# Two blocks of cached attention on one core: the order of the loads on SP's ring

## The chip, the cores and the metric

The kernel runs on one core of one Trainium2 chip. Its engines are named as the profile names them: PE (TensorE), ACT (ScalarE), DVE (VectorE), POOL (GpSimd) and SP (SyncE, which here only issues loads). The metric is the device time of one execution in microseconds. The time before is the median of three runs; one further execution was profiled.

## The reference, cut to what matters

Two problems, A and B, of the same shape and with separate inputs are computed one after the other, and their outputs stand side by side. For each:

```python
# x [16, 144, 448], k_cache and v_cache [16, 16, 512, 256], wq [448, 4096], wo [4096, 448], bf16
q = (x @ wq).reshape(B, Sq, H, Dh).transpose(0, 2, 1, 3)
scores = einsum("bhqd,bhkd->bhqk", q, k_cache) * (Dh ** -0.5)
p = softmax(scores, axis=-1)
o = einsum("bhqk,bhkd->bhqd", p, v_cache)
out = o.transpose(0, 2, 1, 3).reshape(B, Sq, H * Dh) @ wo
```

## The kernel before

The work is cut into 512 **units**, one for each problem, batch and head (256 per problem). For a unit U, PE does Q (L937: eight matmuls, x times the head's columns of wq), S (L961: eight, transposed scores, keys on the partitions), PV (L1007: eight, V times the exponentials) and one matmul with ones that sums the exponentials over the keys (L1019; it occurs once per unit, so that it counts units in the trace). ACT takes the exponential of S (L973) and the reciprocal of the sums as a logarithm and an exponential (L1030, L1035). POOL adds the exponentials of four key blocks to one before the sums matmul (L982, L986). DVE copies Q out of PSUM (L949), reduces the sums to a range flag (L1063) and writes the normalized result into `ring` (L1050), a buffer of four chunks of 128 output rows. The softmax takes no maximum off; the range flag at the end decides whether a second, general program (`_general_path`) runs instead, which these inputs don't need.

The output projection (L1098) takes a chunk of 128 rows of `ring` through all 32 blocks of `wo`, two matmuls at a time, paced by a credit: each unit adds `OP_RATE` matmuls to it, and a chunk can begin `OP_DELAY` units after its last batch is done. ACT copies a finished chunk out (L1116), and POOL stores it (L1127).

Every load is issued by SP, in one order, on one ring. K comes in **groups** of four units (1 MB) by a transposing DMA (`t_load_k`, L913) into one of `NK` slots; V in groups of four units by a plain DMA of 1 MB (`t_load_v`, L922) into one of `NV` slots. x comes for four batches at a time by two transposing DMAs (`t_load_x`, L903 and L904); wq in four pieces of four heads (`t_load_wq`, L882 and L884); wo in eight pieces (`t_load_wo`, L892). Because SP works in order, a load whose slot is not yet free holds up all loads behind it.

The whole program is written out by one loop over steps `i`. In step `i` the loads that are due are issued, and then come Q of unit `i + LQ`, S of unit `i + LS` and PV of unit `i`, followed by pieces of the output projection. Which load is issued in which step is decided by a plan: `plan()` notes for each load the earliest step `lo` (its slot is free), a deadline and a lead; the plan is sorted by deadline, and going through it in that order a load's step is the largest of the step of the load before it, its own `lo`, and its deadline less the lead. A group's K has a deadline two units ahead of its first unit, its V at its first unit; so K and V alternate. The second problem's wo pieces are not in the plan: each is issued when the last projection of problem A that reads the old piece has been written out.

Of the kernel before, what the change touches and what calls it, by code (L numbers as in the profile page):

```python
# [5 lines left out]
BF16 = mybir.dt.bfloat16  # L6
F32 = mybir.dt.float32
# [5 lines left out]
PE, ACT, DVE, POOL, SP = "pe", "act", "dve", "pool", "sp"  # L13
# [110 lines left out]
def _general_path(  # L124
# [45 lines left out]
    RC = RS * 128  # L170
    OP_DELAY = 2
    assert NT % 8 == 0
# [481 lines left out]
    while True:  # L654
# [51 lines left out]
        if 0 <= u < NT:  # L706
# [46 lines left out]
def bass_concat_heads__mha_block_cached__gqa_block_cached__near_ridge_kernel(  # L753
# [37 lines left out]
    assert NWO % WOG == 0 and WOG % OPP == 0 and NT % UG == 0  # L791
    NWG = NWO // WOG

    LQ, LS = 15, 2
    LDQ = SP
    NK, NV, NXG = 5, 4, 3
    XB = 4 if Bn % 4 == 0 else (2 if Bn % 2 == 0 else 1)
    NQT, NPT, NPS, NRI, NOST = 18, 4, 3, 2, 3
    RS = 4
    RC = RS * 128  # L800
    OP_DELAY = 2
    NXGT = NP * Bn // XB
    LIM_EXP = 40

# [2 lines left out]
    with contextlib.ExitStack() as es:  # L807
        mem = contextlib.ExitStack()

        def sb(name, shape, dt):  # L810
            return mem.enter_context(nc.sbuf_tensor(name, shape, dt))
# [14 lines left out]
        ps_sb = sb("ps_sb", [128, NPS, SQ], BF16)  # L826
        ln_sb = sb("ln_sb", [128, NRI, SQ], F32)
        rinv_sb = sb("rinv_sb", [128, NRI, SQ], F32)
        run_sb = sb("run_sb", [1, 2, NT], F32)
        ost_sb = sb("ost_sb", [128, NOST, D], BF16)  # L830
        stat = sb("stat", [128, 4], F32)
        flag_sb = sb("flag_sb", [128, 4], I32)
# [5 lines left out]
        S = _Sched()  # L838
# [38 lines left out]
        def t_load_wq(pr, hg):  # L877
            cols = slice(hg * 4 * DH, (hg + 1) * 4 * DH)
            w = wqs[pr]

            def e(q):
                q.dma_start(wq_sb[:, 0:3, cols], w[0:384, cols].rearrange("(c p) n -> p c n", p=128)).then_inc(  # L882
                    sems["wq%d" % hg], 16)
                return q.dma_start(wq_sb[64:128, 3, cols], w[384:448, cols]).then_inc(sems["wq%d" % hg], 16)  # L884
            S.add(LDQ, e, writes=[(("wq", hg), pr)], dma_sem="wq%d" % hg, n_dma=2, name="wq%d.%d" % (pr, hg))

        def t_load_wo(pr, wg):
            c0 = wg * WOG
            w = wos[pr]

            def e(q):
                return q.dma_start(wo_sb[:, c0:c0 + WOG, :],  # L892
                                   w[c0 * 128:(c0 + WOG) * 128, :].rearrange("(c p) n -> p c n", p=128)).then_inc(
                    sems["wo%d" % wg], 16)
            S.add(LDQ, e, writes=[(("wo", wg), pr)], dma_sem="wo%d" % wg, name="wo%d.%d" % (pr, wg))

        def t_load_x(XG):
            pr, j = divmod(XG, Bn // XB)
# [17 lines left out]
        def t_load_v(G):  # L916
            pr, b, h0 = unit(UG * G)
            sl = G % NV
            src = vs[pr][b, h0:h0 + UG].rearrange("u (p c) d -> p u (c d)", p=128)

            def e(q):
                return q.dma_start(v_sb[:, sl, :, :], src).then_inc(sems["v%d" % sl], 16)  # L922
            S.add(LDQ, e, writes=[(("v", sl), G)], dma_sem="v%d" % sl, name="v%d" % G)

        def t_q(U):
            pr, b, h = unit(U)
# [204 lines left out]
        t_init()  # L1131
        dma_plan = []

        def plan(lo, deadline, lead, fn, *args):
            dma_plan.append((deadline, len(dma_plan), lo, lead, fn, args))

        s_min = -LQ - 24
        for XG in range(NXGT):
            pr, j = divmod(XG, Bn // XB)
            u_first = pr * NU + j * XB * H  # L1140
            dl = u_first - LQ
            if XG >= NXG:
                pr0, j0 = divmod(XG - NXG, Bn // XB)
                lo = pr0 * NU + (j0 + 1) * XB * H - 1 - LQ + 1
            else:
                lo = s_min
            plan(lo, dl, 40, t_load_x, XG)
        for pr in range(NP):
            for hg in range(HG):
                dl = pr * NU + 4 * hg - LQ  # L1150
                lo = pr * NU - H + 4 * hg + 3 - LQ + 3 if pr > 0 else s_min
                plan(lo, dl, 10 ** 6, t_load_wq, pr, hg)
        for wg in range(NWG):
            plan(s_min, H - 4 + 2 * wg, 10 ** 6, t_load_wo, 0, wg)
        for G in range(NG):
            dl = UG * G - LS
            lo = UG * (G - NK) + UG - 1 - LS + 1 if G >= NK else s_min
            plan(lo, dl, 20, t_load_k, G)
        for G in range(NG):
            dl = UG * G  # L1160
            lo = UG * (G - NV) + UG - 1 + 3 if G >= NV else s_min
            plan(lo, dl, 12, t_load_v, G)
        dma_plan.sort(key=lambda t: t[:2])
        _prev = s_min
        _tmp = []
        for dl, sq, lo, lead, fn, args in dma_plan:
# [11 lines left out]
        tail_bank = {}  # L1178
# [5 lines left out]
        fifo = {"op": [], "qp": []}  # L1184
        stores = []
        credit = 0.0
        op_hold = -10 ** 9
        OP_RATE = float(NCH * NWO) / NU
        last_chunk_of = {pr: (pr + 1) * NCH - 1 for pr in range(NP)}
        flag_ev = None  # L1190

        def queue_chunk(r, ready):
            op_first[r], op_last[r] = 0, NWO - 1
            for c in range(NWO):
                fifo["op"].append((r, c, ready))
# [9 lines left out]
        i = s_min  # L1205
        while True:
            while dma_plan and dma_plan[0][0] <= i:
                _sl, _dl, _sq, fn, args = dma_plan.pop(0)
                fn(*args)
            while stores and stores[0][1] <= i:  # L1210
                t_store(stores.pop(0)[0])
            u = i + LQ
            if 0 <= u < NT:
                t_q(u)
                t_evac_q(u)
            u = i + LS
            if 0 <= u < NT:
                t_s(u)
                t_exp(u)
                t_presum(u)  # L1220
            u = i
            if 0 <= u < NT:
                t_pv(u)
                t_sum(u)
                t_recip(u)
                t_check(u)
                t_evac_ot(u)
                pr, b, h = unit(u)
# [113 lines left out]
```

## Time and profile before

| what | value |
|---|---|
| median of three runs | 1164.04 us (1160.04 to 1165.18) |
| the profiled execution, its own time | 1168.88 us |
| its span in the profile | 1167.0 us |
| granted PE clock, mean | 0.983 |
| DMA traffic, mean over the span | 252 GB/s, 294.21 MB |
| K load (transposing), median from issue to landing | 10.8 us (A), 10.6 us (B) |
| V load (plain), median from issue to landing | 6.3 us (A), 6.4 us (B) |

The page gives each engine's busy time as a share of the span. The span is the part of the execution that the trace covers. A wait is put down to the event that ended it. The DMA row of a window cuts it into 40 slices; in a window of 10 us a slice is 0.25 us, and its number is the GB/s that the ring's engines moved in it.

### The profile page before, as it was taken

Reading aid. Unit: us, or ns where it says so; the run is one execution under the profiler, and the core shown is the slowest. Engines: PE = TensorE matmul, PEld = TensorE weight load, DVE = VectorE, ACT = ScalarE, POOL = GpSimd, SP = SyncE. Lnnn points to the kernel's source line nnn. Section 1 sums busy time; section 2 is a strip of 40 time slices with the busy share of each in tenths; the row PEclk is TensorE's granted clock in tenths of the full one; section 3 lists DMA queues with packets and bytes.
Section 4 is the critical chain, followed back from the end, with each engine's and each line's share of the span. In section 5 each row is a group of like instructions: output and inputs, shape, how many; then the busy total and the mean of one; then the engine's idle time right before and its main releaser. Section 6 shows DMA issues by size and latency. Waiting matters only on the chain.

```text
span 1167.0 us, 33127 instructions
## 1 busy us (share of the span) xinstructions
PE 1059.2 (91%) x13952; PEld 928.1 (80%) x13952; DVE 655.6 (56%) x2183; ACT 621.5 (53%) x1573; POOL 642.0 (55%) x1065
## 2 busy tenths in 40 slices
PE   4988899988999989998789878999989998999995
PEld 3877888877897878887678767888878887888874
DVE  2554566555665656665346554666656665666543
ACT  0554556555665655655345444665646565556553
POOL 0554566555665656665346454666656665656553
PEclk9999999999999999999999999999999999999998
DMA  9999999999999999999999999999999999999992
GB/s 233 255 293 259 238 262 255 260 236 257 261 252 248 258 251 268 254 262 259 239 252 269 258 281 256 270 256 257 259 248 258 268 252 243 267 258 257 265 237 75
DMA packets 629087, 294.21 MB, mean 252 GB/s; under 512 B 550464, under 2 KB 558656, under 8 KB 628928
## 3 DMA queue, kind: packets, MB, share of 16 engines
q1 hardware_dynamic: 627200, 287.86, 108.9%
q0 software_dynamic: 1728, 4.13, 1.3%
q8 instruction: 111, 1.82, 0.7%
q14 instruction: 48, 0.39, 0.1%
HBM read 148.90 MB, written 4.13 MB: 131 GB/s over the span
## 4 chain that ended last, share of the span: by engine, by line
PE 57%; DMA 32%; SPq 5%; DVE 3%; ACT 1%; issue 1%; POOLq 0%; POOL 0%; ACTq 0%
DMA kt_sb<-in_B_k_cache_dram 15%; PE s_ps L961 15%; PE qp_ps L937 14%; PE ot_ps L1007 13%; PE op_ps L1098 13%; DMA kt_sb<-in_A_k_cache_dram 10%; DMA v_sb<-in_B_v_cache_dram 3%; SPq L903 2%; SPq L913 2%; PE ot_ps L1019 2%; DMA wq_sb<-in_B_wq_dram 1%; DMA v_sb<-in_A_v_cache_dram 1%; DVE qt_sb L949 1%; ACT pt_sb L973 1%; DVE run_sb L1063 1%
## 5 line engine op out<-in xcount | busy, mean ns | idle before, releaser
L982 POOL TENSOR_TENSOR pp_sb<-pt_sb 128x288 f32<-128x288 bf16 x512 | 373.5, 729 | 470.5 <-ACT pt_sb L973 469.6
L973 ACT ACTIVATE pt_sb<-s_ps 128x576 bf16<-128x576 f32 x512 | 332.8, 650 | 498.4 <-PE s_ps L961 498.4
L1063 DVE TENSOR_REDUCE run_sb<-ot_ps 1x1 f32<-1x144 f32 x1024 | 260.4, 290 | 429.5 <-ACT ln_sb L1030 429.5
L937 PEld LDWEIGHTS qp_ps<-xt_sb,wq_sb 128*128 128x128 bf16 x4096 | 293.0, 100 | 125.0 <-issue 24.9
L937 PE MATMUL qp_ps<-xt_sb,wq_sb 128*128 128x144 bf16 x4096 | 350.9, 231 | 40.5 <-DMA wq_sb<-in_A_wq_dram 11.1
L961 PE MATMUL s_ps<-qt_sb,kt_sb 128*128 128x144 bf16 x4096 | 345.2, 228 | 44.6 <-DMA kt_sb<-in_A_k_cache_dram 25.4
L1007 PE MATMUL ot_ps<-pt_sb,v_sb 128*128 128x144 bf16 x4096 | 343.4, 228 | 10.8 <-DMA v_sb<-in_B_v_cache_dram 7.9
L961 PEld LDWEIGHTS s_ps<-qt_sb,kt_sb 128*128 128x128 bf16 x4096 | 276.0, 99 | 57.0 <-DMA kt_sb<-in_A_k_cache_dram 29.6
L1007 PEld LDWEIGHTS ot_ps<-pt_sb,v_sb 128*128 128x128 bf16 x4096 | 276.7, 98 | 12.7 <-DMA v_sb<-in_B_v_cache_dram 8.7
L1098 PE MATMUL op_ps<-wo_sb,ring 128*128 128x448 bf16 x1120 | 281.9, 356 | 0.5 <-DVE ring L1050 0.5
L986 POOL TENSOR_TENSOR ps_sb<-pp_sb 128x144 bf16<-128x144 f32 x512 | 249.9, 488 | 40.1
L949 DVE CAST qt_sb<-qp_ps 128x288 bf16<-128x288 f32 x512 | 224.9, 439 | 70.1 <-PE qp_ps L937 67.3
L1050 DVE TENSOR_TENSOR ring<-ot_ps,rinv_sb 128x288 bf16<-128x288 f32 (+8 forms) x640 | 230.7, 375 | 0.0
L1035 ACT ACTIVATE rinv_sb<-ln_sb 128x144 f32<-128x144 f32 x512 | 165.4, 323 | 16.2
L1030 ACT ACTIVATE ln_sb<-ot_ps 128x144 f32<-128x144 f32 x512 | 148.6, 290 | 15.8 <-PE ot_ps L1019 15.8
L1098 PEld LDWEIGHTS op_ps<-wo_sb,ring 128*128 128x128 bf16 x1120 | 96.0, 99 | 29.5 <-issue 1.6
L1019 PE MATMUL ot_ps<-ps_sb,ones 128*128 128x144 bf16 x512 | 116.7, 228 | 0.0
L1019 PEld LDWEIGHTS ot_ps<-ps_sb,ones 128*128 128x128 bf16 x512 | 50.4, 98 | 0.0
L1127 POOL DMA_DIRECT2D out_dram<-ost_sb x36 | 20.2, 561 | 4.3 <-ACT ost_sb L1116 4.1
L1116 ACT ACTIVATE ost_sb<-op_ps 128x448 bf16<-128x448 f32 x35 | 18.6, 531 | 3.0 <-PE op_ps L1098 2.6
L1098 PE MATMUL qp_ps<-wo_sb,ring 128*128 128x448 bf16 x32 | 8.2, 353 | 0.0
L1098 PEld LDWEIGHTS qp_ps<-wo_sb,ring 128*128 128x128 bf16 x32 | 3.1, 98 | 2.7
(13 smaller groups left out, 6.1 us busy)
## 6 DMA issues: line engine op xcount, KB each, us to landing
v_sb<-in_A_v_cache_dram SPq DMA_DIRECT2D x64, 1024.0 KB, 6.3
v_sb<-in_B_v_cache_dram SPq DMA_DIRECT2D x64, 1024.0 KB, 6.4
out_dram<-ost_sb POOLq DMA_DIRECT2D x36, 112.0 KB, 6.2
wo_sb<-in_A_wo_dram SPq DMA_DIRECT2D x8, 448.0 KB, 5.9
wo_sb<-in_B_wo_dram SPq DMA_DIRECT2D x8, 448.0 KB, 4.6
wq_sb<-in_A_wq_dram SPq DMA_DIRECT2D x4, 768.0 KB, 8.2
wq_sb<-in_B_wq_dram SPq DMA_DIRECT2D x4, 768.0 KB, 8.5
kt_sb<-in_A_k_cache_dram SPq DMA_TRANSPOSE x64, 10.8
```

Of the source, the lines that this page charges most:

```text
L937: ins = t.matmul(qp_ps[:, dc * SQ:(dc + 1) * SQ], lhsT=wq_sb[:, kc, c0:c0 + 128], rhs=xt_sb[:, xsl, kc, xo:xo + SQ], start=(kc == 0 and dc ...
L949: return v.tensor_copy(qt_sb[:, sl, :, :], src)
L961: ins = t.matmul(s_ps[bank][:, c // 2, (c % 2) * SQ:(c % 2 + 1) * SQ], lhsT=kt_sb[:, ksl, 2 * c + dc, jj * 128:(jj + 1) * 128], rhs=qt_sb[ ...
L973: return a.activation(pt_sb[:, psl, :, :].rearrange("p (a b) q -> p a (b q)", a=2), s_ps[bank][:, :, 0:2 * SQ], AF.Exp, scale=DH ** -0.5)
L982: return g.tensor_tensor(pp_sb[:, sl, :, :], pt_sb[:, psl, 0:2, :], pt_sb[:, psl, 2:4, :], op=ALU.add)
L986: return g.tensor_tensor(ps_sb[:, sl, :], pp_sb[:, sl, 0, :], pp_sb[:, sl, 1, :], op=ALU.add)
L1007: ins = t.matmul(ot_ps[ob][:, dc * SQ:(dc + 1) * SQ], lhsT=v_sb[:, vsl, j, c * DH + dc * 128:c * DH + (dc + 1) * 128], rhs=pt_sb[:, sl, c, ...
L1019: return t.matmul(ot_ps[ob][:, 2 * SQ:3 * SQ], lhsT=ones[:, :], rhs=ps_sb[:, sl, :], start=True, stop=True)
L1035: return a.activation(rinv_sb[:, sl, :], ln, AF.Exp, scale=-1.0)
L1050: ins = v.tensor_tensor(ring[:, 2 * h:2 * h + 2, r0:r0 + q1 - q0], ot_ps[ob][:, 0:2 * SQ].rearrange("p (c q) -> p c q", c=2)[:, :, q0:q1], ...
L1063: return v.tensor_reduce(run_sb[0:1, k, U:U + 1], ot_ps[ob][0:1, 2 * SQ:3 * SQ], axis=AX.X, op=op)
L1098: ins = t.matmul(acc[0:m, 0:D], lhsT=ring[:, c, col0:col0 + m], rhs=wo_sb[:, c, :], start=(c == first), stop=(c == last))
```

## The change

- Loads are issued in waves of four groups (`WAVE = 4`): a K or V load's deadline is that of its wave's first group, and a new sort key, `phase`, puts the wave's K (and x) at 0, wq and V at 1, wo at 2. The groups of the first wave keep deadlines of their own. All leads are so large that only the slots and the order hold a load back.
- K has six slots instead of five, V five instead of four; x two instead of three. Q runs 6 units ahead instead of 15, with 6 slots instead of 18.
- The output projection begins at unit 30 at the earliest (`OP_START`), at 1.15 times the old rate. The first problem's wo pieces are due 12 units before that. Pieces of the last two chunks (those that run beside the last batch) that use the Q bank wait until Q is done.
- Smaller: two staging tiles for the output instead of three, the range flag's values in BF16.

```diff
-    LQ, LS = 15, 2
-    LDQ = SP
-    NK, NV, NXG = 5, 4, 3
+    LQ, LS = 6, 2
+    WAVE = 4
+    NK, NV, NXG = 6, 5, 2
...
-    NQT, NPT, NPS, NRI, NOST = 18, 4, 3, 2, 3
+    NQT, NPT, NPS, NRI, NOST = 6, 4, 3, 2, 2
...
-    OP_DELAY = 2
+    OP_DELAY, OP_START = 2, 30
...
-        run_sb = sb("run_sb", [1, 2, NT], F32)
+        run_sb = sb("run_sb", [1, 2, NT], BF16)
...
-        def plan(lo, deadline, lead, fn, *args):
-            dma_plan.append((deadline, len(dma_plan), lo, lead, fn, args))
+        def plan(lo, deadline, phase, lead, fn, *args):
+            dma_plan.append((deadline, phase, len(dma_plan), lo, lead, fn, args))
...
-            plan(lo, dl, 40, t_load_x, XG)
+            plan(lo, u_first - LQ - 16, 0, 10 ** 6, t_load_x, XG)
...
-                lo = pr * NU - H + 4 * hg + 3 - LQ + 3 if pr > 0 else s_min
-                plan(lo, dl, 10 ** 6, t_load_wq, pr, hg)
+                lo = pr * NU - H + 4 * hg + 3 - LQ + 1 if pr > 0 else s_min
+                plan(lo, dl, 1, 10 ** 6, t_load_wq, pr, hg)
         for wg in range(NWG):
-            plan(s_min, H - 4 + 2 * wg, 10 ** 6, t_load_wo, 0, wg)
+            plan(s_min, OP_START - 12 + wg, 2, 10 ** 6, t_load_wo, 0, wg)
         for G in range(NG):
-            dl = UG * G - LS
             lo = UG * (G - NK) + UG - 1 - LS + 1 if G >= NK else s_min
-            plan(lo, dl, 20, t_load_k, G)
+            w = 1 if G < WAVE else WAVE
+            plan(lo, UG * (G - G % w) - LS, 0, 10 ** 6, t_load_k, G)
         for G in range(NG):
-            dl = UG * G
-            lo = UG * (G - NV) + UG - 1 + 3 if G >= NV else s_min
-            plan(lo, dl, 12, t_load_v, G)
-        dma_plan.sort(key=lambda t: t[:2])
+            lo = UG * (G - NV) + UG - 1 + 1 if G >= NV else s_min
+            w = 1 if G < WAVE else WAVE
+            plan(lo, UG * (G - G % w) - LS, 1, 10 ** 6, t_load_v, G)
+        dma_plan.sort(key=lambda t: t[:3])
...
-        OP_RATE = float(NCH * NWO) / NU
+        OP_RATE = 1.15 * NCH * NWO / NU
...
-                            fifo[tail_bank[r]].append((r, 2 * h + dc, i + 1))
+                            ready = i + 1 if tail_bank[r] == "op" else max(i + 1, NT - LQ)
+                            fifo[tail_bank[r]].append((r, 2 * h + dc, ready))
...
-                            queue_chunk(r, i + OP_DELAY)
+                            queue_chunk(r, max(i + OP_DELAY, OP_START))
```

What this makes of SP's order is shown at three places. The first is the start of the program: after x, SP issues wq (two DMAs a piece), K (`kt_sb`) and V (`v_sb`). Before:

```order
L903 DMA_TRANSPOSE xt_sb<-in_A_x_dram 128x3x576
L904 DMA_TRANSPOSE xt_sb<-in_A_x_dram 128x576
L882 DMA wq_sb<-in_A_wq_dram 128x3x1024
L884 DMA wq_sb<-in_A_wq_dram 64x1024
L882 DMA wq_sb<-in_A_wq_dram 128x3x1024
L884 DMA wq_sb<-in_A_wq_dram 64x1024
L882 DMA wq_sb<-in_A_wq_dram 128x3x1024
L884 DMA wq_sb<-in_A_wq_dram 64x1024
L882 DMA wq_sb<-in_A_wq_dram 128x3x1024
L884 DMA wq_sb<-in_A_wq_dram 64x1024
L913 DMA_TRANSPOSE kt_sb<-in_A_k_cache_dram 128x8x512
L922 DMA v_sb<-in_A_v_cache_dram 128x4x1024
```

The same place in the changed kernel:

```order
L903 DMA_TRANSPOSE xt_sb<-in_A_x_dram 128x3x576
L904 DMA_TRANSPOSE xt_sb<-in_A_x_dram 128x576
L882 DMA wq_sb<-in_A_wq_dram 128x3x1024
L884 DMA wq_sb<-in_A_wq_dram 64x1024
L913 DMA_TRANSPOSE kt_sb<-in_A_k_cache_dram 128x8x512
L882 DMA wq_sb<-in_A_wq_dram 128x3x1024
L884 DMA wq_sb<-in_A_wq_dram 64x1024
L922 DMA v_sb<-in_A_v_cache_dram 128x4x1024
L913 DMA_TRANSPOSE kt_sb<-in_A_k_cache_dram 128x8x512
L882 DMA wq_sb<-in_A_wq_dram 128x3x1024
L884 DMA wq_sb<-in_A_wq_dram 64x1024
L922 DMA v_sb<-in_A_v_cache_dram 128x4x1024
```

The first K moves ahead of three of the four wq pieces, and each of these is then followed by a V and a K.

The second place is SP in the middle of problem A, ahead of and behind a load of x; `waits s_pe` marks a load that waits until PE has finished reading the slot. Before:

```order
L904 DMA_TRANSPOSE xt_sb<-in_A_x_dram 128x576
L913 DMA_TRANSPOSE kt_sb<-in_A_k_cache_dram 128x8x512
L922 DMA v_sb<-in_A_v_cache_dram 128x4x1024 [waits s_pe]
L913 DMA_TRANSPOSE kt_sb<-in_A_k_cache_dram 128x8x512
L922 DMA v_sb<-in_A_v_cache_dram 128x4x1024 [waits s_pe]
```

In the changed kernel:

```order
L922 DMA v_sb<-in_A_v_cache_dram 128x4x1024 x2
L922 DMA v_sb<-in_A_v_cache_dram 128x4x1024 [waits s_pe] x2
L903 DMA_TRANSPOSE xt_sb<-in_A_x_dram 128x3x576
L904 DMA_TRANSPOSE xt_sb<-in_A_x_dram 128x576
L913 DMA_TRANSPOSE kt_sb<-in_A_k_cache_dram 128x8x512
L913 DMA_TRANSPOSE kt_sb<-in_A_k_cache_dram 128x8x512 [waits s_pe] x3
```

Four transposes now stand together, and then four plain loads; the wait on PE's slots, which stood at every V, stands at three K and two V of a wave.

The third place is SP in problem B, where the first of B's wo pieces comes in. Before:

```order
L913 DMA_TRANSPOSE kt_sb<-in_B_k_cache_dram 128x8x512
L892 DMA wo_sb<-in_B_wo_dram 128x4x448 [waits s_pe]
L922 DMA v_sb<-in_B_v_cache_dram 128x4x1024
L913 DMA_TRANSPOSE kt_sb<-in_B_k_cache_dram 128x8x512
L892 DMA wo_sb<-in_B_wo_dram 128x4x448 [waits s_pe] x2
L922 DMA v_sb<-in_B_v_cache_dram 128x4x1024
```

In the changed kernel:

```order
L892 DMA wo_sb<-in_B_wo_dram 128x4x448 [waits s_pe]
L922 DMA v_sb<-in_B_v_cache_dram 128x4x1024
L913 DMA_TRANSPOSE kt_sb<-in_B_k_cache_dram 128x8x512
L892 DMA wo_sb<-in_B_wo_dram 128x4x448 [waits s_pe]
L913 DMA_TRANSPOSE kt_sb<-in_B_k_cache_dram 128x8x512 [waits s_pe]
L892 DMA wo_sb<-in_B_wo_dram 128x4x448 [waits s_pe] x3
L913 DMA_TRANSPOSE kt_sb<-in_B_k_cache_dram 128x8x512
L892 DMA wo_sb<-in_B_wo_dram 128x4x448 [waits s_pe] x3
L913 DMA_TRANSPOSE kt_sb<-in_B_k_cache_dram 128x8x512
```

Before, the wo pieces came just ahead of a V, so that they added no change from transposing to plain loads; now they stand between the K of one wave, and all of that wave's V come behind them.

More of the change, by code (lines that the diff above doesn't have):

```diff
@@ L884, in e @@
                 return q.dma_start(wq_sb[64:128, 3, cols], w[384:448, cols]).then_inc(sems["wq%d" % hg], 16)
-            S.add(LDQ, e, writes=[(("wq", hg), pr)], dma_sem="wq%d" % hg, n_dma=2, name="wq%d.%d" % (pr, hg))
+            S.add(SP, e, writes=[(("wq", hg), pr)], dma_sem="wq%d" % hg, n_dma=2, name="wq%d.%d" % (pr, hg))
         def t_load_wo(pr, wg):
@@ L894, in e @@
                     sems["wo%d" % wg], 16)
-            S.add(LDQ, e, writes=[(("wo", wg), pr)], dma_sem="wo%d" % wg, name="wo%d.%d" % (pr, wg))
+            S.add(SP, e, writes=[(("wo", wg), pr)], dma_sem="wo%d" % wg, name="wo%d.%d" % (pr, wg))
         def t_load_x(XG):
@@ L922, in e @@
                 return q.dma_start(v_sb[:, sl, :, :], src).then_inc(sems["v%d" % sl], 16)
-            S.add(LDQ, e, writes=[(("v", sl), G)], dma_sem="v%d" % sl, name="v%d" % G)
+            S.add(SP, e, writes=[(("v", sl), G)], dma_sem="v%d" % sl, name="v%d" % G)
         def t_q(U):
@@ L1132, in bass_concat_heads__mha_block_cached__gqa_block_cached__near_ridge_kernel, with wave @@
         dma_plan = []
-        def plan(lo, deadline, lead, fn, *args):
-            dma_plan.append((deadline, len(dma_plan), lo, lead, fn, args))
+        def plan(lo, deadline, phase, lead, fn, *args):
+            dma_plan.append((deadline, phase, len(dma_plan), lo, lead, fn, args))
         s_min = -LQ - 24
+        def wave(G):
+            return UG * (G - G % WAVE)
         for XG in range(NXGT):
@@ L1140, in bass_concat_heads__mha_block_cached__gqa_block_cached__near_ridge_kernel @@
             u_first = pr * NU + j * XB * H
-            dl = u_first - LQ
             if XG >= NXG:
@@ L1150, in bass_concat_heads__mha_block_cached__gqa_block_cached__near_ridge_kernel @@
                 dl = pr * NU + 4 * hg - LQ
-                lo = pr * NU - H + 4 * hg + 3 - LQ + 3 if pr > 0 else s_min
-                plan(lo, dl, 10 ** 6, t_load_wq, pr, hg)
+                lo = pr * NU - H + 4 * hg + 3 - LQ + 1 if pr > 0 else s_min
+                plan(lo, dl, 1, 10 ** 6, t_load_wq, pr, hg)
         for wg in range(NWG):
-            plan(s_min, H - 4 + 2 * wg, 10 ** 6, t_load_wo, 0, wg)
+            plan(s_min, OP_START - 12 + wg, 2, 10 ** 6, t_load_wo, 0, wg)
         for G in range(NG):
-            dl = UG * G - LS
             lo = UG * (G - NK) + UG - 1 - LS + 1 if G >= NK else s_min
-            plan(lo, dl, 20, t_load_k, G)
+            w = 1 if G < WAVE else WAVE
+            plan(lo, UG * (G - G % w) - LS, 0, 10 ** 6, t_load_k, G)
         for G in range(NG):
-            dl = UG * G
-            lo = UG * (G - NV) + UG - 1 + 3 if G >= NV else s_min
-            plan(lo, dl, 12, t_load_v, G)
-        dma_plan.sort(key=lambda t: t[:2])
+            lo = UG * (G - NV) + UG - 1 + 1 if G >= NV else s_min
+            w = 1 if G < WAVE else WAVE
+            plan(lo, UG * (G - G % w) - LS, 1, 10 ** 6, t_load_v, G)
+        dma_plan.sort(key=lambda t: t[:3])
         _prev = s_min
         _tmp = []
-        for dl, sq, lo, lead, fn, args in dma_plan:
+        for dl, ph, sq, lo, lead, fn, args in dma_plan:
             _prev = max(_prev, lo, dl - lead)
```

## The prediction

> **What bounds the kernel now.** I read the busy shares first, then the waits of PE, then the DMA traffic in windows of 10 us.
>
> ```profile
> PE 1059.2 (91%) x13952; PEld 928.1 (80%) x13952; DVE 655.6 (56%) x2183; ACT 621.5 (53%) x1573; POOL 642.0 (55%) x1065
> q1 hardware_dynamic: 627200, 287.86, 108.9%
> ...
> PE s_ps L961 <- DMA kt_sb<-in_A_k_cache_dram: 25.4, 19, 3.1
> PE s_ps L961 <- DMA kt_sb<-in_B_k_cache_dram: 18.6, 22, 2.7
> PE qp_ps L937 <- DMA wq_sb<-in_A_wq_dram: 11.1, 1, 11.1
> PE qp_ps L937 <- DMA wq_sb<-in_B_wq_dram: 9.8, 3, 6.5
> PE qp_ps L937 <- DVE qt_sb L949: 8.1, 19, 0.6
> PE ot_ps L1007 <- DMA v_sb<-in_B_v_cache_dram: 7.9, 4, 3.2
> ```
>
> Two resources are nearly full: TensorE, and the ring that SP feeds, whose packets are in flight all the time. PE's waits end on K above all, not on another engine. How much is lost in which stretch is counted in the sums matmuls (L1019, one per unit); the columns are the stretch, its length, PE busy (count), PEld busy (count), granted clock, DMA share and GB/s:
>
> ```profile
> 67.30:108.20 40.90, 3.86 (x17) 1.71 (x17) 0.96 1.13 277
> 108.20:1153.00 1044.80, 109.03 (x479) 47.05 (x478) 0.99 1.13 254
> 1153.00:1167.00 14.00, 0.23 (x1) 0.10 (x1) 0.64 0.08 23
> 782.50:814.30 31.80, 3.62 (x16) 1.53 (x16) 1.00 1.14 266
> 549.80:602.30 52.50, 3.92 (x17) 1.72 (x17) 0.90 1.11 244
> 636.00:677.70 41.70, 3.73 (x16) 1.64 (x17) 0.96 1.15 264
> ```
>
> An undisturbed stretch of 16 units takes 31.8 us, 1.99 us a unit. So 479 units should take 952 us, and they take 1044.8: **93 us** are lost after the start. 20 of them go where problem B's query weights come in (52.5), 10 where its output weights do (41.7), the rest in small K waits. A wait costs more than its length, since the clock falls after it (0.56 and 0.59 here, PE idle from 100 to 102):
>
> ```profile
> 100.00:102.00 2.00, 0.00 (x0) 0.00 (x0) 1.09 (x4) 0.18 (x1) 0.91 (x2) 1.00 1.10 330
> 102.00:104.00 2.00, 1.63 (x14) 1.64 (x15) 0.00 (x0) 0.45 (x1) 0.00 (x0) 0.56 1.03 356
> 104.00:106.00 2.00, 2.00 (x21) 2.00 (x20) 1.05 (x4) 0.81 (x3) 1.22 (x2) 0.59 1.25 239
> ```
>
> What does one K and one V cost the ring? SP's issues (start, length), and the GB/s in slices of 0.25 us from 106 to 116 us:
>
> ```profile
> 99.72 7.06 SPq L913 DMA_TRANSPOSE kt_sb<-in_A_k_cache_dram  x1
> 106.83 0.58 SPq L922 DMA_DIRECT2D v_sb<-in_A_v_cache_dram  x1
> 107.45 7.03 SPq L913 DMA_TRANSPOSE kt_sb<-in_A_k_cache_dram  x1
> ...
> 115.15 8.78 SPq L913 DMA_TRANSPOSE kt_sb<-in_A_k_cache_dram  x1
> GB/s 289 290 291 292 290 288 293 289 213 23 33 197 147 295 246 377 410 410 401 369 418 377 339 308 284 100 24 273 291 293 292 285 292 292 288 289 295 287 290 239
> ```
>
> The period from K issue to K issue is 7.7 us. In the row K runs flat at 290 GB/s (1.05 MB: 3.6 us), then a hole (213 23 33 197 147), V at some 370 (3 us), another hole (100 24), K again. Against 290 the first hole loses 0.7 us, the second 0.4: **1.1 us per pair of switches**. There is also a longer hole that is not tied to a switch:
>
> ```profile
> GB/s 254 410 401 336 369 303 270 336 360 360 353 274 237 98 257 287 293 291 290 288 292 291 288 293 291 289 233 158 32 32 151 322 290 344 394 356 311 202 221 295
> GB/s 323 269 212 13 0 5 8 10 93 288 292 289 291 329 289 221 252 101 271 108 167 236 102 289 193 197 385 393 393 393 393 451 369 369 360 210 282 57 8 16
> GB/s 289 330 258 75 0 2 9 10 52 280 275 270 292 289 290 290 294 286 292 292 289 289 291 271 188 246 139 33 164 369 410 418 377 369 377 418 378 310 289 117
> ```
>
> The first two are the first (40 to 50 us) and the last (1110 to 1120) of 108 such rows. In them I counted 325 stretches under 215 GB/s; 62 lose over 1.15 us each (like 13 0 5 8 10), 88 us together, several in the middle of a K. I take those as staying. Check: a wave of four K and four V now takes 4 x 7.7 + 2.6 (88 us over 34 waves of 31.8 us) = 33.4 us; 30 waves after unit 32 make 1002, and x (7 times 0.59 MB, 2 us and a hole, 3 us), four wq and eight wo (24, by the prices below) some 45 more: 1047 us against the 1044.8 seen. **The ring sets the pace now**, PE (952) follows.
>
> **The change, part by part.** (1) *Waves.* Of four pairs of switches one is left: 33.4 - 3 x 1.1 = 30.1 us a wave, 903 for 30, 948 with the 45. Whether two transposes in a row leave a hole, the old order shows only at x (L903, L904, then K; last row above, 140 to 150): from L904 into K the flow is unbroken, 142.25 to 146; between L903 and L904 stands a hole of 1.4 us, of the long kind. Per K-to-K seam the bounds are thus 0 and 1.4 us; I take 0, the row nearest to a whole K. SP can feed it, as K issues as short as 4.07 us occur against 3.6 of flow:
>
> ```profile
> L913 SPq DMA_TRANSPOSE kt_sb<-in_A_k_cache_dram x64: 4067/7306/12931, 8.8 to 573.2; - x64
> ```
>
> (2) *The new waits.* In units counted from a wave's first: its fourth K waits for the S of the group three before it, done at step -11 (S runs 2 ahead); behind it in SP's queue stand the four V, and behind the fourth V (its slot comes free at -4) the next K. From -11 the K issue (7.3) and a V landing (6.3) end 13.6 us or 7 units later, at -4: 8 us before PE needs that V. The ring has some idle time there. So the slot waits cost nothing, unless a wave is over 8 us late.
>
> ```profile
> v_sb<-in_A_v_cache_dram SPq DMA_DIRECT2D x64, 1024.0 KB, 6.3
> ```
>
> (3) *The start.* Five Q instead of fourteen stand ahead of the first S, and Q runs cold there (1.69 us each, 11.07 to 12.74). But the ring decides:
>
> ```profile
> GB/s 0 0 0 0 0 0 0 0 0 58 144 231 187 289 293 289 274 180 169 162 145 45 90 180 180 295 352 369 360 352 320 344 287 197 172 197 262 320 393 303
> GB/s 295 336 336 385 352 311 188 221 254 270 262 385 270 287 393 377 369 303 188 156 238 262 262 393 311 238 352 369 361 325 213 162 179 143 164 93 56 51 16 47
> 11.07 1.12 PE L937 MATMUL qp_ps<-xt_sb,wq_sb 128*128 128x144 bf16 x8 [11.07 <-DMA wq_sb<-in_A_wq_dram]
> 12.74 1.14 PE L937 MATMUL qp_ps<-xt_sb,wq_sb 128*128 128x144 bf16 x8 [0.55 <-DVE qt_sb L949]
> 38.20 7.17 SPq L913 DMA_TRANSPOSE kt_sb<-in_A_k_cache_dram  x1
> ...
> 90.50 0.58 SPq L922 DMA_DIRECT2D v_sb<-in_A_v_cache_dram  x1
> ```
>
> In the rows of 0 to 10 and 10 to 20 us, x ends at 5.2 and the four wq at 18.5: 3.3 us each. From 38.20 to 90.50 go five K, five V and eight wo: 52.3 - 38.5 leaves 1.7 us a wo (I take 1.4, since some of it is PE's pace). New ledger: x and wq0 to 9.5 (with a hole); K0 to 13.5; wq1 with V0 to 19.7; K1 to 24; wq2 with V1 to 30; K2, wq3 with V2 to 40; K3, V3 to 48; four K to 66 (with 3 us of long holes); V4 lands at 71, V7 at 78; eight wo to 89; four K to 107; **V8 lands at 112**. PE has done unit 31 by 104 (71 + 16 units of 1.70, below, + 32 projection matmuls of 0.19, which stand together at unit 30) and waits. Unit 32 then stands at 113, against 108.2 now.
>
> (4) *PE's own work.* Nine Q that were done ahead are still to come: 9 x 0.5 (41.02 - 40.51) = 4.5 us. The faster output rate (1.15) bunches the projection: by the instruction order 188 of the first 496 units carry none, against 101. Such a unit waits for DVE before its Q:
>
> ```profile
> 40.51 0.67 PE L937 MATMUL qp_ps<-xt_sb,wq_sb 128*128 128x144 bf16 x8
> 41.02 0.66 PE L961 MATMUL s_ps<-qt_sb,kt_sb 128*128 128x144 bf16 x8
> ...
> 43.90 0.68 PE L937 MATMUL qp_ps<-xt_sb,wq_sb 128*128 128x144 bf16 x8
> 76.63 0.54 PE L1098 MATMUL op_ps<-wo_sb,ring 128*128 128x448 bf16 x2
> 77.01 0.66 PE L937 MATMUL qp_ps<-xt_sb,wq_sb 128*128 128x144 bf16 x8
> ...
> 78.57 0.54 PE L1098 MATMUL op_ps<-wo_sb,ring 128*128 128x448 bf16 x2
> ```
>
> Two units without projection take 3.39 us, 1.70 each; with it 1.94 less its two matmuls (0.38) is 1.56. So 0.135 x 78 units after the start = 10.5 us.
>
> (5) *Into problem B.* wq0 goes behind V63, wq1 between K67 and V64, wq2 and wq3 behind V67; wo in pieces between K72 and K75, so V72 waits behind four more switches and 11 us of wo. By the ledger's prices wq2 comes 3 us late and V72 some 10, against 20 and 10 lost now. With 7 us for the first waves, whose V has no lead yet, I put **20 us** of stalls (bounds 5 and 45).
>
> (6) The rest costs nothing: x two groups deep instead of three is loaded 16 units early; the staging tile of two waits for a store issued two chunks (some 28 units) earlier; the flag in BF16 is an operand of 1024 short reductions on a DVE that is 56% busy. Without that cover: at most their length.
>
> **The sum**, on the profiled execution: 113 + 952 + 4.5 + 10.5 + 20 + 14 (the tail row) = 1114 of span, where 1167.0 stood. It ran 1168.88 us, 1.9 beyond its span and 4.8 above the median of the runs; 1116 in the same ratio is **1111 us**.
>
> **Rivals.** *A: the holes belong to the transfers, not to the switches.* Then a wave still costs 33.4, the ring still sets the pace, and only the start moves (+5): 1172 of span, 1169 us. For it: 62 holes have nothing to do with a switch. Against it: the short ones sit where the rate changes. The Trainium skill, "DMA: Bandwidth & Descriptors", on HWDGE ordering under "Queues, rings and completion order", says that descriptors go in ring order and that data descriptors carry no barrier. By that rule a switch costs nothing and A holds; the trace's 23 and 33 GB/s between K and V speak against it.
>
> *B: a seam between two transposes leaves a hole, as between L903 and L904 at 140.75.* Three seams a wave at 1.4 us make 34.3 us: 30 x 34.3 + 45 + 127 = 1201, or 1198 us, slower. It decides from 1.0 us per seam, where a wave reaches the 33.2 that the old span allows. Against it: the unbroken flow from L904 into K.
>
> *C: the ring gains, PE does not see it*, because V arrives at the end of each wave and margins of 8 us are eaten by double holes; stalls of 45 instead of 20 give 1136 us.
>
> **How the numbers follow.** Forecast 0.50 (own range 1085 to 1125), C 0.14, a cheaper start 0.05, A 0.18, B 0.13. 0.5% is about what a measurement of this kernel can tell from no change. Faster by more (below 1158): the first three, 0.69. A lies just inside the upper edge of no change (1170): 0.16 of it to same, 0.02 to slower. Slower: B and that rest, 0.15. The range, 1085 to 1172, reaches from the forecast over C to A; B and the cheaper start lie outside.
>
> **What would show it.** Right: the GB/s rows at 0.25 us show some 15 us flat at 290, one hole, 12 us at 350 to 400; K waits of PE fall from 44 to under 15 us; 16 units take 32 to 33 us from 120 us on; unit 32 stands near 113. Wrong: holes between K and K (B), a wave of 33 us (A), PE waiting for the first V of waves in mid-run (C), or a start later than 120.

## The result, and the profile after

The changed kernel takes **1131.22 us** (median of four runs, 1130.3 to 1134.42) against 1164.61 for the kernel before on the same chip (four runs, 1160.04 to 1165.37): a ratio of 0.9726, 95% interval 0.9694 to 0.9758. The forecast was 1111 us, so of 53 us some 33 came. The profiled execution took 1134.42 us, with a span of 1132.7.

From the page of the changed kernel: the busy engines, SP's ring, and PE's waits on a DMA (us in total, times, longest):

```profile
PE 1050.6 (93%) x13952; PEld 925.9 (82%) x13952; DVE 657.6 (58%) x2183; ACT 621.8 (55%) x1573; POOL 643.4 (57%) x1065
q1 hardware_dynamic: 627200, 287.86, 107.5%
...
PE ot_ps L1007 <- DMA v_sb<-in_A_v_cache_dram: 22.1, 5, 12.7
PE qp_ps L937 <- DMA wq_sb<-in_A_wq_dram: 16.9, 3, 10.6
PE qp_ps L937 <- DMA wq_sb<-in_B_wq_dram: 10.9, 2, 7.4
PE ot_ps L1007 <- DMA v_sb<-in_B_v_cache_dram: 7.1, 3, 4.3
PE s_ps L961 <- DMA kt_sb<-in_A_k_cache_dram: 1.6, 1, 1.6
```

The 44 us that PE waited for K are 1.6. What is left are waits for wq and V at the start, and for wq and V around the change to problem B. Where the span goes is read again from the sums matmuls (L1019), cut at units 32, 240, 320 and the last; before, units 240 and 320 stood at 549.82 and 750.72.

```profile
115.38:538.68 423.30, 47.11 (x209) 20.36 (x209) 1.00 1.15 269
538.68:725.31 186.63, 18.38 (x81) 8.03 (x81) 0.95 1.13 273
725.31:1118.06 392.75, 43.17 (x192) 18.69 (x192) 1.00 1.05 250
```

Units 32 to 511 take 1002.7 us where they took 1045.1; the start gives 7 us of that back (unit 32 at 115.38, before at 108.06). The first and the third stretch now run at full granted clock: PE sets the pace there. The second, the **change of problem**, has a clock of 0.95 and holds most of the loss. Cut at each 16 units from unit 240 on:

```profile
538.68:580.35 41.67, 3.72 (x17) 1.66 (x17) 0.88 1.12 291
580.35:620.01 39.66, 3.71 (x16) 1.61 (x17) 0.96 1.13 285
620.01:657.54 37.53, 3.62 (x17) 1.63 (x17) 1.00 1.17 259
657.54:693.72 36.18, 3.72 (x17) 1.56 (x17) 0.96 1.11 258
693.72:725.31 31.59, 3.62 (x17) 1.57 (x17) 1.00 1.13 269
```

Four steps of 36 to 42 us where the steps around them take 32 to 34. PE's instructions there that waited for a DMA (start, length, and in brackets the idle time before them and who ended it), and SP's issues around the first wq:

```profile
538.17 0.24 PE L1007 MATMUL ot_ps<-pt_sb,v_sb 128*128 128x144 bf16 x1 [1.88 <-DMA v_sb<-in_A_v_cache_dram]
572.95 0.28 PE L937 MATMUL qp_ps<-xt_sb,wq_sb 128*128 128x144 bf16 x1 [7.41 <-DMA wq_sb<-in_B_wq_dram]
588.19 0.22 PE L937 MATMUL qp_ps<-xt_sb,wq_sb 128*128 128x144 bf16 x1 [3.51 <-DMA wq_sb<-in_B_wq_dram]
656.91 0.24 PE L1007 MATMUL ot_ps<-pt_sb,v_sb 128*128 128x144 bf16 x1 [4.29 <-DMA v_sb<-in_B_v_cache_dram]
693.21 0.24 PE L1007 MATMUL ot_ps<-pt_sb,v_sb 128*128 128x144 bf16 x1 [2.29 <-DMA v_sb<-in_B_v_cache_dram]
```

```profile
532.15 3.74 SPq L922 DMA_DIRECT2D v_sb<-in_A_v_cache_dram  x4
535.93 1.43 SPq L882 DMA_DIRECT2D wq_sb<-in_B_wq_dram  x1
537.40 1.83 SPq L884 DMA_DIRECT2D wq_sb<-in_B_wq_dram  x1
539.27 27.29 SPq L913 DMA_TRANSPOSE kt_sb<-in_B_k_cache_dram  x4
566.60 0.59 SPq L882 DMA_DIRECT2D wq_sb<-in_B_wq_dram  x1
```

wq1 is issued at 566.60, when PE is already waiting for it (since 565.54 = 572.95 - 7.41): four K stand ahead of it in SP's order.

What a wave looks like on the ring. SP's K issues, all of one problem (min/median/max ns), and the GB/s in slices of 0.25 us from 90 to 100 us (the end of wo, then K after K) and from 440 to 450 (the end of four V, then K):

```profile
L913 SPq DMA_TRANSPOSE kt_sb<-in_A_k_cache_dram x64: 4049/4847/16002, 5.0 to 527.4; - x64
```

```profile
GB/s 368 315 298 116 49 33 19 108 295 289 288 292 291 288 290 294 290 287 293 290 168 139 162 161 34 11 9 24 284 289 292 290 290 291 291 288 291 291 291 288
GB/s 385 385 401 393 385 401 426 393 393 393 393 401 410 385 401 393 385 362 289 293 167 52 42 41 25 15 134 290 290 291 288 293 289 292 288 292 291 288 291 224
```

K is not 15 us flat at 290: around the end of the first K stands a hole (168 139 162 161 34 11 9 24), and the median issue is 4.85 us for 3.6 us of flow, some 1.2 us more. Not all of this is a **seam**, a loss between one K and the next. In this hole the trace has a packet of the queue that brings instructions, which starts at 95.04 (the last section); in the 1 us from 95 to 96 the view of the DMA queues lists it:

```profile
q8 instruction: 1, 0.02, 6.7%
```

How much is seam can be counted in e9 (below), where the ring sets the pace. There the bytes of one K and of the next begin 4.4 us apart on average where no such packet falls in (63 pairs), and 5.3 us apart where one does (21 pairs). So the **seam of two K is some 0.8 us**, and the rest comes with the instructions. V, however, runs at about 400 GB/s when it comes four in a row, 2.6 us each, against the 3 us that it took between two K.

### The profile page after: what moved, and what is told of

Its sections match the earlier page's. It is cut to its first block, busy times and chain, and to the rows that moved or that the text cites. A ratio compares the mean times of both kernels' runs of the same rounds, so it can differ in the third digit from the quotient of the medians.

```text
span 1132.7 us, 33125 instructions
## 1 busy us (share of the span) xinstructions
PE 1050.6 (93%) x13952; PEld 925.9 (82%) x13952; DVE 657.6 (58%) x2183; ACT 621.8 (55%) x1573; POOL 643.4 (57%) x1065
## 4 chain that ended last, share of the span: by engine, by line
PE 74%; DVE 7%; DMA 7%; SPq 6%; ACT 5%; issue 1%; POOLq 0%; POOL 0%; ACTq 0%
PE qp_ps L937 19%; PE op_ps L1098 18%; PE s_ps L961 18%; PE ot_ps L1007 16%; SPq L913 5%; ACT pt_sb L973 4%; DVE run_sb L1063 3%; DMA v_sb<-in_A_v_cache_dram 3%; DVE ring L1050 2%; DVE qt_sb L949 2%; PE ot_ps L1019 2%; DMA v_sb<-in_B_v_cache_dram 2%; DMA wq_sb<-in_B_wq_dram 1%; ACT ln_sb L1030 1%; DMA kt_sb<-in_A_k_cache_dram 1%
## 5 line engine op out<-in xcount | busy, mean ns | idle before, releaser
L1063 DVE TENSOR_REDUCE run_sb<-ot_ps 1x1 bf16<-1x144 f32 x1024 | 262.2, 293 | 376.5 <-ACT ln_sb L1030 376.5
L937 PE MATMUL qp_ps<-xt_sb,wq_sb 128*128 128x144 bf16 x4096 | 347.3, 229 | 38.6 <-DMA wq_sb<-in_A_wq_dram 16.9
L937 PEld LDWEIGHTS qp_ps<-xt_sb,wq_sb 128*128 128x128 bf16 x4096 | 284.3, 99 | 113.2 <-issue 29.7
L1098 PE MATMUL op_ps<-wo_sb,ring 128*128 128x448 bf16 x1120 | 265.5, 353 | 0.5 <-DVE ring L1050 0.5
L1019 PE MATMUL ot_ps<-ps_sb,ones 128*128 128x144 bf16 x512 | 116.3, 227 | 0.0
L1019 PEld LDWEIGHTS ot_ps<-ps_sb,ones 128*128 128x128 bf16 x512 | 50.5, 99 | 0.0
```

The source lines that it names most:

```text
L937: ins = t.matmul(qp_ps[:, dc * SQ:(dc + 1) * SQ], lhsT=wq_sb[:, kc, c0:c0 + 128], rhs=xt_sb[:, xsl, kc, xo:xo + SQ], start=(kc == 0 and dc ...
L1019: return t.matmul(ot_ps[ob][:, 2 * SQ:3 * SQ], lhsT=ones[:, :], rhs=ps_sb[:, sl, :], start=True, stop=True)
L1063: return v.tensor_reduce(run_sb[0:1, k, U:U + 1], ot_ps[ob][0:1, 2 * SQ:3 * SQ], axis=AX.X, op=op)
L1098: ins = t.matmul(acc[0:m, 0:D], lhsT=ring[:, c, col0:col0 + m], rhs=wo_sb[:, c, :], start=(c == first), stop=(c == last))
```

## The experiments

Each is compared with the kernel before on the same chip. "Units 32 to 511" is read from the profiled execution as above.

**e1: waves of one.** Everything of the change but the grouping.

```diff
-    WAVE = 4
+    WAVE = 1
```

> The changed kernel (1131 us) with waves of one group: K and V alternate again, with the new numbers of slots (6 K, 5 V, 2 x), Q 6 ahead and the new output projection. Theory (the gain is the switches between transposing and plain loads, and the ring sets the pace without it): a wave of the ring costs some 33 us again, PE waits for K or V in mid-run, 16 units take 34 to 35 us, 1155 to 1175 us. Rival (the gain comes from the slots, the reach of Q and the projection): 1125 to 1140 us.

1164.26 us (ten runs), ratio 1.0008 (0.9978 to 1.0038). Its three stretches, and its waits on a DMA:

```profile
108.11:550.39 442.28, 47.11 (x209) 20.41 (x209) 1.00 1.14 255
550.39:748.12 197.73, 18.38 (x81) 8.07 (x81) 0.93 1.14 268
748.12:1146.78 398.66, 43.16 (x191) 18.69 (x192) 1.00 1.10 250
```

```profile
PE s_ps L961 <- DMA kt_sb<-in_A_k_cache_dram: 32.4, 20, 5.5
PE qp_ps L937 <- DMA wq_sb<-in_A_wq_dram: 17.3, 4, 10.8
PE op_ps L1098 <- DMA wo_sb<-in_B_wo_dram: 14.9, 3, 5.4
PE s_ps L961 <- DMA kt_sb<-in_B_k_cache_dram: 5.3, 7, 1.3
```

The K waits are back, 37.7 us. More slots, the shorter reach of Q, the later and faster projection gain nothing by themselves: the whole gain hangs on the grouping. Whether grouping would gain as much without them was not tried.

**e2: waves of two** (`WAVE = 2`).

> The changed kernel with waves of two groups: two pairs of switches per four groups where the change has one and the old order four. Theory (switches): some 31 us of ring per four groups, still under PE's 32, so most of the gain stays: 1128 to 1145 us. Rival (only the slots matter): the same as waves of one. If long waves have a price of their own (V at the end of the wave is late), two is faster than four: under 1128 us.

1132.56 us (1129.92 to 1134.93), ratio 0.9726 (0.9678 to 0.9774): the same as four. Unit 32 comes earlier (110.0), but units 240 to 320 take 192.2 us instead of 186.6. Two K in a row are enough to let PE set the pace; what remains is at the ends.

**e5 and e6: no V, no K.** e5 loads V for the first five groups only, e6 K for the first six; later units use what lies in the slots. All else is computed.

```diff
-        for G in range(NG):
+        for G in range(NV):
```

> The changed kernel with V loaded for the first five groups only; the later units use those five again (left out: 123 of 128 V loads). It shows PE without a ring that limits it, and K alone on the ring. Theory (from unit 32 on PE is the bound outside the change of problem): the steps of 16 units stay at 31.8 to 32.1 us, the start and the change of problem lose much less, 1070 to 1090 us. The long holes (1.4 us with 7 to 11 GB/s in them) still come at multiples of some 256 PE instructions, in the middle of a K too, if they belong to something that PE's progress triggers; if they belong to switches between K and V they are gone.

> The changed kernel with K loaded for the first six groups only (left out: 122 of 128 K loads); V alone on the ring. The same PE program, so as in the kernel without V some 1070 to 1090 us. If the long holes need a transpose in flight, they are gone from the ring although PE runs the same instructions; if they stop any transfer, they stay.

1096.82 and 1088.21 us (one execution each). Units 32 to 511 of e5, and of e6:

```profile
107.10:1081.02 973.92, 108.25 (x479) 46.85 (x480) 1.00 0.69 141
```

```profile
98.64:1072.57 973.93, 108.25 (x479) 46.86 (x480) 1.00 0.44 142
```

Twice the same: **974 us is PE's own floor** for these units, with no wait for a load in it. The changed kernel takes 1002.7, so 28.7 us of stalls are left in it. The same three stretches of e6:

```profile
98.64:517.60 418.96, 47.01 (x209) 20.35 (x209) 1.00 0.45 143
517.60:680.52 162.92, 18.08 (x80) 7.82 (x81) 1.00 0.55 178
680.52:1072.57 392.05, 43.17 (x191) 18.69 (x192) 1.00 0.39 126
```

Against it the changed kernel loses 4.3 us in the first, **23.7 in the second**, 0.7 in the third.

**e9 and e10: the ring by itself.** PE's work is cut (two of Q's eight matmuls, four of S's, two of PV's eight are done), so that it no longer sets the pace; every transfer stays. e9 with waves of four, e10 with waves of one.

```diff
-                    for c in range(4):
+                    for c in range(1):
```

> PE's work is cut (2 of the 8 matmuls of Q, 4 of the 8 of S, 2 of the 8 of PV), all transfers and their order stay, in waves of four; so the ring alone sets the pace and the time of 128 units is that of 8 waves. If four V in a row pay for the seams between the K (K 4.9 us each as in the start, V 10.3 us for four), a wave is 30 to 31.5 us and 480 units after unit 32 take 900 to 990 us with x and the weights; if a wave were as dear as four single pairs (33 us and more), they take as long as in the sister run with waves of one, within 1%.

> The same cut of PE's work, with waves of one. If the switches cost the ring 1.1 us a pair (the prediction's figure), this runs 30 x 3.3 = some 100 us longer than the run with waves of four; if the seams between K take back a part (1.2 us each, three a wave, against four V at 2.55 instead of 3.03 us each), the two differ by some 30 to 50 us; if order made no difference for the ring alone, by under 10 us, and the gain of the change would then have to come from when V and K arrive, not from the ring's capacity.

1083.12 and 1112.82 us (one execution each). Units 32 to 511, and 48 to 96, which is three waves without an x in them; of e9 also 16 units with an x and 16 without. e9:

```profile
113.20:1067.72 954.52, 117.99 (x480) 51.89 (x480) 0.82 1.11 275
146.52:237.21 90.69, 11.46 (x49) 5.01 (x49) 0.86 1.13 282
...
237.21:271.40 34.19, 4.02 (x16) 1.72 (x17) 0.75 1.14 269
146.52:177.10 30.58, 3.81 (x16) 1.67 (x17) 0.89 1.14 277
```

e10:

```profile
106.31:1097.47 991.16, 124.17 (x480) 55.21 (x480) 0.81 1.11 266
136.23:234.50 98.27, 13.02 (x48) 5.87 (x49) 0.78 1.12 260
```

In these three waves the ring takes 30.2 us a wave grouped (90.69 / 3) and 32.8 ungrouped (98.27 / 3). Over the whole run the difference is smaller: 991.16 - 954.52 = 36.6 us over 30 waves, so **1.2 us saved per wave**, and the three waves overstate it. That is the middle expectation (30 to 50 us), and well under the 3 x 1.1 us a wave that the prediction took. The saving comes from V. Counted from the first byte of one load to that of the next, where no packet of instructions falls in, a V before a V takes 3.0 us on average (e9) and a V before a K 3.7 (e10); a K before a K takes 4.4 (e9), which is more than the 4.1 of a K before a V (e10).

**e3, e7, e8, e12: can the change of problem be relieved?** e3 loads B's first four groups one by one, so that wq1 to wq3 come between them. e7 does this too, holds B's wo back until V of the wave is out, and lets B's first projection begin 44 units into B at the earliest. e8 does so with waves of two, at most three pieces of wo in each run of V, and 40 units. e12 uses single groups, then waves of two in problem A, and waves of four in B. Of e3 and of e12:

```diff
-            w = 1 if G < WAVE else WAVE
+            w = 1 if G % (NG // NP) < WAVE else WAVE
```

```diff
-            w = 1 if G < WAVE else WAVE
+            w = 1 if G < 4 else (2 if G < NG // NP else WAVE)
```

And of e7, where `wo_pend` collects the pieces (e8 has `min(3, ...)`):

```diff
+                if fn is t_load_v and wo_pend and not (dma_plan and dma_plan[0][3] is t_load_v):
+                    for _ in range(min(8, len(wo_pend))):
+                        t_load_wo(*wo_pend.pop(0))
...
-                                t_load_wo(pr + 1, c // WOG)
+                                wo_pend.append((pr + 1, c // WOG))
```

> The changed kernel with the first wave of problem B loaded group by group, as problem A's first wave is, so that each piece of wq stands behind one K and not behind four. Theory (29 us are lost in the 64 units around the change of problem because the wq pieces stand behind a whole wave's K): the waits for wq of B fall from 10.9 to under 4 us, the 64 units from 155 to some 140 us, 1115 to 1125 us. Rival (the traffic itself is too much there, wherever it stands): PE waits for K or V instead, 1128 to 1135 us.

> The kernel with problem B's first wave loaded group by group, and beside that B's wo pieces held back until the V of the wave are issued, eight at most in a row, with B's first output projection 44 units into B. Theory (the wo pieces between the K of a wave make V late there): the steps 272 and 288 (42 us each without this) lose less, 1118 to 1128 us. Rival (the ring has no room for the weights in those 64 units, wherever they stand): 1130 to 1136 us, the loss moves again.

> Waves of two groups, problem B's first four groups one by one, B's wo pieces held back until a V phase and at most three of them at a time, B's first output projection 40 units into B. Theory (the weights must be spread over more time than the ring lags): steps 240 to 304 together 140 us instead of 155, 1115 to 1122 us. Rival (no room, wherever they stand): 1128 to 1136 us.

> Problem A in waves of two (after four single groups), problem B in waves of four. With waves of two throughout unit 224 came some 9 us earlier than with waves of four, and was lost again at the change of problem. If the change of problem costs the same 29 us whatever stands before it, this takes about 1122 us; rival: the ring is the limit up to there, what PE gains before it is waited for at B's weights, and the time stays at 1129 to 1134 us.

| kernel | us (range) | ratio to before (interval) | units 240 to 320 | longest waits at B |
|---|---|---|---|---|
| changed | 1131.22 (1130.3 to 1134.42) | 0.9726 (0.9694 to 0.9758) | 186.6 | wq 7.4, V 4.3 |
| e3 | 1133.91 (1129.44 to 1135.11) | 0.973 (0.9682 to 0.9778) | 182.6 | V 7.7 |
| e7 | 1130.96 (1128.93 to 1132.75) | 0.9697 (0.9662 to 0.9732) | 188.0 | V 10.4 |
| e8 | 1151.83 (1151.28 to 1152.26) | 0.9878 (0.9845 to 0.991) | 209.1 | wo 16.4 |
| e12 | 1139.45 (1136.27 to 1145.6) | 0.9794 (0.976 to 0.9827) | 193.7 | wq 15.0 |

e3 shows how the loss moves. Its steps of 16 units from unit 240 on:

```profile
539.33:571.19 31.86, 3.62 (x17) 1.57 (x17) 1.00 1.14 297
571.19:613.58 42.39, 3.62 (x17) 1.62 (x17) 0.92 1.15 264
613.58:655.88 42.30, 3.72 (x17) 1.66 (x17) 0.94 1.12 293
655.88:689.71 33.83, 3.72 (x17) 1.56 (x17) 0.97 1.16 260
```

The wait for wq is gone and the first step is clean; the next two take 42 us each, and PE waits 17.8 us for V instead of 7.1. Its units 240 to 320 are 4 us shorter than the change's, but units 320 to 511 take 397.7 us instead of 392.8. e7 moves it on (two steps of 45 us), e8 held wo back so long that PE waited 16.4 us for it. e12 came to the change of problem with unit 240 at 534.85 instead of 538.68, and gave it back there (wq 15.0): the 1122 us that it should have had if B's price were fixed did not come, and it is even slower than its rival's 1129 to 1134. No order of the same transfers that was tried beats the change by more than the intervals.

**e11: B's weights not loaded.** Problem B uses A's wq and wo; nothing else differs.

> The loads of problem B's wq and wo are left out (A's stand in), all else as in the changed kernel. If the 29 us lost between units 240 and 320 are the weights' traffic on the ring, these steps fall to 32 to 33 us each and the time to 1102 to 1108 us. Rival: they come from the larger group of x and V that falls there anyway, or from PE's own order; then the time stays above 1120 us.

1109.39 us (1106.31 to 1112.45), ratio 0.9519 (0.9479 to 0.9559): 22 us less than the change, just short of what was expected. Its three stretches:

```profile
115.37:539.38 424.01, 47.11 (x209) 20.34 (x209) 1.00 1.15 270
539.38:702.30 162.92, 18.08 (x81) 7.82 (x81) 1.00 1.15 269
702.30:1094.93 392.63, 43.17 (x192) 18.70 (x192) 1.00 1.04 248
```

Units 240 to 320 take 162.92 us, to the hundredth what they take without K in e6. So all 23.7 us come with the 7.3 MB of weights, and none with x, V or PE's order alone.

**e4: the projection at its old rate** (`OP_RATE` without the 1.15).

> The changed kernel with the output projection at its old rate (1.0). Theory of the prediction (a unit without projection costs 0.135 us in a wait for DVE): fewer such units, 3 to 10 us faster, 1121 to 1128 us. Rival (these waits cost nothing, or the slower rate delays the second problem's wo pieces): 1129 us or more.

1133.34 us (1127.53 to 1143.55), ratio 0.9767 (0.9704 to 0.983). In its profiled execution, the fastest of the four, units 32 to 511 take 997.5 us instead of 1002.7; the times are too far apart to tell it from the change.

## Why the prediction came out as it did

The sum, term by term; the measured values are those of the profiled execution, with PE's floor from e6:

| term | predicted | measured |
|---|---|---|
| unit 32 | 113 | 115.4 |
| PE's own, units 32 to 511 (952 + 4.5 + 10.5) | 967 | 973.9 |
| stalls, units 32 to 240 (the first waves, in the prediction) | 7 | 4.3 |
| stalls at the change of problem | 13 | 23.7 |
| stalls after it | 0 | 0.7 |
| after the last unit | 14 | 14.6 |
| span | 1114 | 1132.7 |

- **The mechanism was right.** The ring set the pace, grouping makes a wave cheaper for it, and PE takes over. e1 has all but the grouping and stays at 1164; in the changed kernel 16 units take 32 us at a granted clock of 1.00, and the K waits are gone. Rival A (holes belong to the transfers; 1169) falls with this: by e9 and e10 a wave does get cheaper. The rule of the Trainium skill that was weighed for it ("DMA: Bandwidth & Descriptors", HWDGE ordering under "Queues, rings and completion order") names ring order without barriers; nothing in it would make the 1.2 us a wave by which e9 and e10 differ.
- **The price of a wave came out by luck.** 30.1 us were predicted, and e9's three waves took 30.2. But the predicted figure holds all long holes of the old kernel (2.6 us a wave), and e9, with fewer PE instructions, has 24 of them where the changed kernel has 41 (counts in the last section). By 17 more holes of 1.4 us over 30 waves the full kernel's wave is some 31.0 us, an estimate. And grouping takes 1.2 us from a wave, not 3 x 1.1: the K-to-K seam, taken as 0, is some 0.8 us, three times a wave, which a faster V more than pays for. The seam is rival B's sign, but it stays under the 1.0 us from which B was to decide. The hole of 1.4 us that B was drawn from is not a seam of two transposes: in the kernel before, a packet of instructions starts at 140.28, just ahead of it.
- **The step that failed is the fifth, into problem B: 13 us predicted, 23.7 measured.** The ledger's price of the weights on the ring was right: with PE out of the way, units 240 to 320 of e9 take 177.7 us, which is 23 more than five waves and one x (5 x 30.2 + 3.6), and 24 was the ledger's sum. Wrong was the part of it that PE would be spared. The prediction had wq2 3 us late and V72 10; the waits are 7.4 and 3.5 on wq, 4.3 and 2.3 on V, and the granted clock of the 16 units with the longest of them is 0.88. A ring at 31 us a wave beside a PE at 32 has 1 us a wave to spare, not 2, and the slots let it run ahead by little: where PE waits for a wave's first V in mid-run, it is behind an x, by 0.2 to 1.9 us, and an x costs the ring some 3.6 us (e9's 16 units with one take 34.19, against 30.58 without). By the landings in the trace, the first V of a wave is there 1.6 us ahead of its use in the median of 23 waves (units 64 to 224 and from 320 on), and never more than 6.0, where **step 2 had 8 us**. Nearly every microsecond of weights is therefore one of stall: they cost the ring 23 us and PE 23.7, which e11 gives back whole; and by e3, e7, e8 and e12 another order only chooses who waits.
- **PE's own work** was 7 us too low, 967 against 973.9, because its added terms were counted against the old kernel and not against the stretches of 31.8 us that gave the 952. (The stretch shown in the prediction is cut 1.1 us short, its 16 units take 32.9; but units 192 to 208 and 320 to 336 do take 31.8.) Such a stretch carries 36 projection matmuls, loses nothing in units without projection, and has a Q in every unit. In e6, units 32 to 510 hold 159 units without projection, each some 0.12 us longer than the trend of the others (two projection matmuls more, 0.38 us more) would make it: 19 us, not the 10.5 of the 78 that are new. Units 32 to 510 carry 1112 projection matmuls, 34 more than at 36 in 16 units, at 0.19 us each: 6 us. And the last six of them have no Q: 3 us less, where the prediction added 4.5 for Q that the 952 already holds. Together 974 to 975, an estimate.
- **The start** was 2.4 us off, at the wait for V8 (PE idle 6.5 us, until 114.45), as the ledger had it.
- **What was to cost nothing** (step 6: fewer x and staging slots, the flag in BF16) cost nothing that shows: e1 has it all and stands at 1.0008 of the kernel before. A small cost to PE would not show there, since PE waits for K in e1.
- **Rival C** (PE waits for the first V; 1136 us) is near in time, and its premise, that the margin of 8 us is eaten, was right. What was to follow from it came to little: waits for a wave's first V in mid-run are 3.4 us in all, at four places. That the 1132.7 us of span lie between forecast and C is the work of the terms above: B's weights, which the thin margin made dear, and PE's own work.

Open: what the remaining 0.8 us between two transposes are made of, and whether part of the 23.7 us can be had by loading B's weights earlier into space of their own, which the kernel does not have.

## What to carry to other kernels

Where one ring carries transposing and plain loads, two of a kind in a row gave as much as four here: group until the compute engine sets the pace, then stop. Once ring and compute engine are within a few per cent, look for the one place with extra traffic (here new weights), and count all of it as stall unless the trace shows the lead that would hide it. Price a new neighbourhood of transfers from that very pair, or leave the price open; here 3.3 us a wave were forecast for the grouping and 1.2 measured, and errors that cancelled hid it.

## What the runs showed of the hardware

**The long holes come with packets of instructions.** The holes of 1.4 us with 5 to 11 GB/s in them, which the prediction took as not tied to a switch, were counted between 110 and 1080 us, against PE's matmuls and weight loads. Counted are stretches under 100 GB/s, at most 2 us long, with at least two slices of 7 to 11 GB/s, which is fewer than all that are as long:

```
kernel            PE instructions   long holes
before                27904             42
changed               27904             41
e1 (waves of one)     27904             50
e9, e10 (PE cut)      11520           24, 24
e5 (no V)             27904             27
e6 (no K)             27904              3
```

The page lists a queue that brings instructions; of the changed kernel, and of e9:

```profile
q8 instruction: 111, 1.82, 0.7%
```

```profile
q8 instruction: 47, 0.77, 0.3%
```

Packets of 16 KB, one for some 256 PE instructions (27904 / 256 = 109, 11520 / 256 = 45). The trace has the time of each. In the changed kernel 31 of the 41 holes begin within 1 us of a packet's start; of 98 packets in these 970 us, some 8 would by chance. In the kernel before, the middle 70% of the bytes of a K take 2.54 us in the median, and 4.01 us where a packet starts in them or just ahead (84 and 33 loads); those of a V take 2.06 and 2.20 us (107 and 10 loads). Without K the holes are all but gone, though PE runs as many instructions. So a hole goes with a packet of instructions while a transpose is in flight, and costs the transpose some 1.5 us. That the packet causes the hole was not tried by itself: no run took the packets away and left PE's work as it was.

**Transposing loads are slower than plain ones.** K flows at 290 GB/s, V in a row at about 400. The Trainium skill, "Advanced Engine Details and Errata", "X-Bar Transpose (TRN2)", has transposes as fast as regular transfers; here they were not in any row shown.
